# Idle matmuls, y on GpSimd, PSUM copies on ScalarE and reordered loads in an mLSTM cell followed by a max-out MLP

## The chip, the cores and the metric

The kernel runs on one core of a Trainium2 chip. Times are device microseconds of that core (us; ns where marked). A run is called fast or slow by its state: slow is a run more than 1.5% above the fastest run of the same kernel. Ratios are the mean time of one kernel's fast runs over that of the other's of the same rounds, so they are not quite the ratio of the medians that are quoted beside them. The ratios of the experiments leave out each kernel's profiled run and judge fast without it.

A matmul is called cold here when it runs at about half rate: 512-column matmuls then start about 427 ns apart, against about 216 ns warm. Some matmul records are missing from a trace, so a group of seven can stand for eight.

Engines are named as the profile names them: PE (TensorE matmuls), PEld (its weight loads), DVE (VectorE), ACT (ScalarE), POOL (GpSimd), SP (SyncE, which issues most DMAs here).

## The reference

There are two parts. The first is a recurrent attention cell (an mLSTM) for 4 batches, 8 heads, 768 steps and head size 40. Its output, reshaped to 3072 rows of 320, goes through a max-out MLP.

```python
for t in range(S):
    m_new = max(f_t + m, i_t)
    C = exp(f_t + m - m_new) * C + exp(i_t - m_new) * outer(v_t, k_t)
    n = exp(f_t + m - m_new) * n + exp(i_t - m_new) * k_t
    y_t = sigmoid(o_t) * (C @ q_t) / max(abs(n . q_t), 1)
x = y.reshape(3072, 320)
out = max(x @ w1, x @ w2) @ w_out          # w1, w2: 320x1024, w_out: 1024x320
```

## The kernel before

The kernel uses that the gates make the state constant after a short head of the sequence. It checks this on the data (`check_gates`) and would run a general version otherwise. Tokens are handled in 12 pairs of 128-token tiles. For each pair: q is cast to bf16 (`cast_q`), transposed on PE (`q_trans`), multiplied with the state (`h_pair`), scaled to y, and y is transposed (`y_trans`) to give xT. The MLP uses max(a, b) = relu(a - b) + b: `moe_u` multiplies xT with w1 - w2 and ACT takes the relu into `gt`; `moe_out` multiplies `gt` with w_out and adds xT times Wc = w2 @ w_out, which `w2_trans` and `wc_mm` prepare.

All instructions stand in the program's order on each engine. The parts that matter here:

```python
def h_pair(b, c0, P=None):                 # cut: ph = state x q on PE, two PSUM tiles
    for j in range(2):
        den = max(-ph[:, :, D], ...)       # DVE
        t = (sig + 1) * ph                 # DVE
        den = max(ph[:, :, D], den); rec = 1 / den                  # DVE
        nc.vector.tensor_tensor(out=y[:, j, 0:DM], in0=t, in1=rec, op=OP.mult)
    nc.vector.tensor_copy(out=y[:, :, DM:DM + 64], in_=y[:, :, DM - 64:DM])

def check_gates():                         # cut
    # DVE scan of f -> F; POOL a = i - F; DVE reduce of a; DVE ok_b
    nc.tensor.matmul(pf, ok_b, ones_b)     # PE: all 32 rows fine?
    # DVE: flag, flag_i

load_batch(1)                              # k, v, q, o of batch 1
...
cast_w2(0); cast_w2(1)                     # POOL
load_batch(2)                              # no store stands in the queue yet
...
load_batch(3)
...
for j, (g, half) in enumerate(steps):      # the loop: 10 steps, two outputs each
    moe_u(g, half, (2 + 2 * j, 3 + 2 * j))
    # y_trans of pair j+5; moe_out; h_pair of pair j+6; moe_out; q_trans of pair j+7
    # ACT: cast_q and gate_o of pair j+8
    if j == 4:
        check_gates()
```

PSUM tiles of the cell come from a pool of two buffers (`pp_f`), `gt` has two buffers, staged q and o have two buffers each.

Of the kernel before, what the change touches and what calls it, by code (L numbers as in the profile page):

```python
# [8 lines left out]
FP = mybir.dt.float32  # L9
BF = mybir.dt.bfloat16  # L10
# [7 lines left out]
def kernel(  # L18
# [100 lines left out]

    def load_qo(b, src, store, name, eng, rest):  # L120
        if b not in store:
            store[b] = stg.tile([128, H, NT, D], FP, name=name, tag=name)
        t = store[b]
        if not rest:
            eng.dma_start(out=t[:, :, 0, :], in_=src[b, :, 0:L, :].rearrange("h p d -> p h d"))
        else:
            eng.dma_start(out=t[:, :, 1:NT, :].rearrange("p h c d -> p h (c d)"),
                          in_=src[b, :, L:S, :].rearrange("h (p c) d -> p h (c d)", c=REST))

# [38 lines left out]
    def state_k(b):  # L168
        pk = pp_f.tile([3 * D, 3, SR], BF, name="pk", tag="pf")
        for tr in range(3):  # L170
            nc.tensor.transpose(pk[:, tr, :], kblk[:, b, tr].rearrange("p a b -> p (a b)"), ident_b[0:SR, 0:SR])  # L171
        kT[b] = ewp.tile([3 * D, 3, SR], BF, name="kT", tag="kT", bufs=2)
        nc.vector.tensor_copy(out=kT[b], in_=pk)

# [27 lines left out]
    def h_pair(b, c0, P=None):  # L202
# [15 lines left out]
        for j in range(2):  # L218
            c, ph = c0 + j, phs[j]
            den = ewp.tile([128, H], FP, name="den", tag="den")  # L220
            if c == 0:
                nc.vector.scalar_tensor_tensor(out=den, in0=ph[:, :, D], scalar=-1.0,
                                               in1=flT[:, b * H:(b + 1) * H], op0=OP.mult, op1=OP.max)
            else:
                nc.vector.tensor_scalar(out=den, in0=ph[:, :, D], scalar1=-1.0, scalar2=2.0,
                                        op0=OP.mult, op1=OP.max)
            t = ewp.tile([128, H, D], FP, name="t", tag="t")
            nc.vector.scalar_tensor_tensor(out=t, in0=sig[b][:, c], scalar=1.0, in1=ph[:, :, 0:D],  # L228
                                           op0=OP.add, op1=OP.mult)
            nc.vector.tensor_tensor(out=den, in0=ph[:, :, D], in1=den, op=OP.max)  # L230
            rec = ewp.tile([128, H], FP, name="rec", tag="rec")
            nc.vector.reciprocal(out=rec, in_=den)  # L232
            nc.vector.tensor_tensor(out=y[:, j, 0:DM].rearrange("p (h d) -> p h d", d=D), in0=t,  # L233
                                    in1=rec.unsqueeze(2).to_broadcast([128, H, D]), op=OP.mult)
        nc.vector.tensor_copy(out=y[:, :, DM:DM + 64], in_=y[:, :, DM - 64:DM])
        return y
# [5 lines left out]

    def y_trans(n0, y):
        g = group_of[n0]
        s0, m = n0 - GROUPS[g][0], GROUPS[g][1]
        if g not in xT:
            xT[g] = xtp.tile([128, 3, m * L], BF, name="xT", tag="xT")
        py = pp_f.tile([128, 3, 2 * L], BF, name="py", tag="pf")
        for j in range(2):
            for c in range(3):  # L250
                nc.tensor.transpose(py[:, c, j * L:(j + 1) * L], y[:, j, c * 128:(c + 1) * 128], ident_b)  # L251
        nc.vector.tensor_copy(out=xT[g][:, :, s0 * L:(s0 + 2) * L], in_=py)  # L252

# [58 lines left out]
    def diff_x(half):  # L312
        s = slice(half * 512, half * 512 + 512)
        for r in (slice(0, 64), slice(64, 128)):
            nc.vector.tensor_tensor(out=wd2[r, s], in0=wx_st[half, 0], in1=wx_st[half, 1], op=OP.subtract)

# [9 lines left out]
    def w2_trans():  # L326
        for c in range(2):
            pw = pp_o.tile([128, NFF, 128], BF, name="pw", tag="po")
            for f in range(NFF):
                nc.tensor.transpose(pw[:, f, :], w2b[:, c, f * 128:(f + 1) * 128], ident_b)  # L330
            nc.vector.tensor_copy(out=w2T[:, c], in_=pw)
        pw = pp_f.tile([128, NFF, 64], BF, name="pwx", tag="pf")
# [18 lines left out]
    def check_gates():  # L351
# [7 lines left out]
                                op0=OP.add, op1=OP.is_ge)  # L359
        nc.vector.tensor_tensor(out=ok_b, in0=viol[:, 1:2], in1=viol[:, 2:3], op=OP.mult)  # L360
        pf = pp_f.tile([1, 1], FP, name="pf", tag="pf")
        nc.tensor.matmul(pf, ok_b, ones_b, start=True, stop=True)
        nc.vector.tensor_scalar(out=flag, in0=pf, scalar1=BH - 0.5, scalar2=None, op0=OP.is_lt)
        nc.vector.tensor_copy(out=flag_i, in_=flag)



    nc.gpsimd.memset(kst[:, :, 2, :], 0.0)
    nc.gpsimd.memset(vst[:, :, 2, :], 0.0)
    nc.vector.memset(warm, 0.0)  # L370
    load_qo(0, q, qst, "qst", nc.scalar, False)
    load_qo(0, q, qst, "qst", nc.scalar, True)
    nc.scalar.activation(out=warm, in_=warm, func=AF.Exp)
    load_gates(0, L)
    load_kv(0, k, kst)
    load_kv(0, v, vst)
    load_qo(0, o_gate, ost, "ost", nc.sync, False)
    load_qo(0, o_gate, ost, "ost", nc.sync, True)
    for half in range(2):
        load_wx(half)  # L380
        load_w(half, 0)
        load_w(half, 1)
    wo_st = wst.tile([128, NFF, DM], FP, name="wo_st", tag="wo_st")
    nc.sync.dma_start(out=wo_st, in_=moe_w_out.rearrange("(f p) m -> p f m", p=128))

    def load_batch(b):
        load_kv(b, k, kst)
        load_kv(b, v, vst)
        for rest in (False, True):
            load_qo(b, q, qst, "qst", nc.sync, rest)  # L390
        for rest in (False, True):
            load_qo(b, o_gate, ost, "ost", nc.sync, rest)

    load_batch(1)
    load_gates(L, S)


    make_identity(nc, ident_b)
    make_identity(nc, ident_f)
    nc.vector.memset(one1, 1.0)  # L400
# [8 lines left out]
    nc.gpsimd.tensor_copy(out=bmk[:, 2, 1:3], in_=bm[:, 2, 0:2])  # L409
    nc.vector.memset(sel, 1.0)  # L410
    for base, cm, step, tstep in ((0, 1, -T0, 0), (T0 - 1, -1, T0, 0), (0, -1, T0, 1)):
        nc.gpsimd.affine_select(out=sel, in_=sel, compare_op=OP.is_ge, fill=0.0, base=base,
                                pattern=[[step, 3], [tstep, 128]], channel_multiplier=cm)

# [10 lines left out]
    cast_q(0, 0, 1, nc.scalar)  # L425
    prep_k(0, nc.vector)
    nc.vector.tensor_tensor(out=sel[:, 0], in0=sel[:, 0], in1=sel[:, 1], op=OP.max)
    nc.vector.tensor_tensor(out=mask, in0=sel[:, 0], in1=sel[:, 2], op=OP.max)
    state_k(0)
    pg = pp_f.tile([128, 2, BH], FP, name="pg", tag="pf")  # L430
# [6 lines left out]
    prep_v(0, nc.vector)  # L437
    state_c(0)


    cast_q(0, 1, 2, nc.scalar)
    q_trans(0, 0)
    P = scores(0)
    cast_q(0, 2, 4, nc.scalar)
    cast_q(0, 4, 6, nc.scalar)
    gate_o(0, 0, 1)
    gate_o(0, 1, 2)
    gate_o(0, 2, 4)
    gate_o(0, 4, 6)
    q_trans(0, 2)  # L450
    q_trans(0, 4)
    y0 = h_pair(0, 0, P)
    y1 = h_pair(0, 2)
    diff_x(0)
    y_trans(0, y0)
    diff(0, 0)
    diff(0, 1)
    y_trans(2, y1)
    y2 = h_pair(0, 4)
    moe_u(0, 0)  # L460
    y_trans(4, y2)
    diff_x(1)
    diff(1, 0)
    diff(1, 1)
    moe_u(1, 0)
    moe_u(0, 1)
    moe_u(1, 1)
    cast_w2(0)
    cast_w2(1)
    nc.vector.tensor_copy(out=wo, in_=wo_st)  # L470
    load_batch(2)
    prep_k(1, nc.gpsimd)
    prep_v(1, nc.gpsimd)
    cast_q(1, 0, 2, nc.scalar)
    cast_q(1, 2, 4, nc.scalar)
    cast_q(1, 4, 6, nc.scalar)
    gate_o(1, 0, 2)
    gate_o(1, 2, 4)
    gate_o(1, 4, 6)
    load_batch(3)  # L480
    w2_trans()
    wc_mm()
    state_k(1)
    state_c(1)
    q_trans(1, 0)
    open_outs((0, 1))
    moe_out(0)
    P = scores(1)
    q_trans(1, 2)
    y3 = h_pair(1, 0, P)  # L490
    moe_out(1)
    y4 = h_pair(1, 2)
    q_trans(1, 4)


    ys = {3: y3, 4: y4}
    cast_q(2, 0, 2, nc.scalar)
    y_trans(6, ys.pop(3))
    ys[5] = h_pair(1, 4)
    gate_o(2, 0, 2)  # L500
    y_trans(8, ys.pop(4))
    prep_k(2, nc.gpsimd)
    prep_v(2, nc.gpsimd)
    q_trans(2, 0)
    state_k(2)
# [4 lines left out]
    def place(p):  # L510
        return 2 * p // NT, 2 * p % NT

    steps = [(g, half) for g in range(2, len(GROUPS)) for half in range(2)]
    for j, (g, half) in enumerate(steps):
        moe_u(g, half, (2 + 2 * j, 3 + 2 * j))
        py_, ph_, pq_ = j + 5, j + 6, j + 7
# [7 lines left out]
        if pq_ < 12 and place(pq_)[1] == 0:  # L524
            state_k(place(pq_)[0])
        moe_out(2 + 2 * j)
        if ph_ < 12:
            ys[ph_] = h_pair(b, c, P)
        moe_out(3 + 2 * j)
        if pq_ < 12:  # L530
# [11 lines left out]
        if j == 4:  # L542
            check_gates()
    open_outs((22, 23))
    moe_out(22)
# [137 lines left out]
```

## Time and profile before

| | before |
|---|---|
| time, median of the first 3 runs | 141.1 us (140.52 to 147.07) |
| span of the profiled run | 139.7 us |
| PE, DVE, ACT, POOL busy | 97.0, 69.2, 51.3, 14.8 us |
| first wide expert matmul | 26.4 us |
| start of the loop | 61.4 us |
| end of the last matmul | 134.1 us |

The profiled run took 141.35 us.

The following lines are from the page of the kernel before: span, busy times, then four rows of 40 equal slices of the span (3.5 us each, counted from 0 in this text). Digits are tenths: the busy share of PE and DVE, the granted PE clock, and the mean busy share of the 16 DMA engines.

```profile
span 139.7 us, 2028 instructions
...
PE 97.0 (69%) x727; PEld 59.6 (43%) x735; DVE 69.2 (50%) x208; ACT 51.3 (37%) x82; POOL 14.8 (11%) x31
...
PE   0027532586678882579789999995059999999940
...
DVE  3455899939143599952726675748530640000000
...
PEclk9999999999999999658999999999955999999999
DMA  4949999896798981000021111112000112022221
...
```

PE is hardly busy in the first 8 us and has a hole at slice 28. The clock row dips twice: slices 16 to 18 (56 to 66 us) and 29 to 30 (101 to 108 us). DVE is at 9 in slices 5 to 7 (17 to 28 us) and 14 to 16 (49 to 59 us), where PE is not.

The next lines are from the windows view of the kernel before. After the window and its length stand busy time and count of PE, PEld, DVE, ACT and POOL, then clock, DMA share and GB/s.

```profile
...
15.00:26.00 11.00, 3.86 (x27) 2.38 (x28) 10.61 (x31) 0.02 (x1) 2.83 (x5) 1.00 1.03 296
47.00:61.00 14.00, 9.01 (x81) 6.51 (x81) 11.92 (x42) 3.36 (x6) 0.00 (x0) 0.87 0.40 116
...
```

DVE binds in both stretches: 10.6 of 11.0 us and 11.9 of 14.0 us.

From the wait table of the kernel before (engine, what it issued, whom it waited for: us in total, times, longest):

```profile
...
ACT gt L293 <- PE po L302: 14.0, 1, 14.0
...
PE pf L362 <- DVE ok_b L360: 6.2, 1, 6.2
...
```

ACT could not write `gt` because its buffer was still read by the matmuls of output 3, and PE stood 6.2 us before the flag matmul `pf`.

From the timeline of the kernel before, PE only (start, duration, engine, line, operation, tiles, count, and the idle time before with what ended it):

```profile
...
26.39 3.19 PE L278 MATMUL pu<-xT,wd 128*128 128x512 bf16 x7 [0.22 <-issue]
...
61.38 3.00 PE L278 MATMUL pu<-xT,wd 128*128 128x512 bf16 x7 [0.22 <-issue]
...
```

Seven 512-column matmuls take 3.19 us at 26.4 and 3.00 us at 61.4, about 430 to 460 ns each. In the warm part of the loop eight take about 1.9 us. Another window of the same timeline shows the gate check:

```profile
...
97.80 1.53 DVE L352 TENSOR_TENSOR_SCAN F<-one_100,F,f_sb 32x640 f32<-32x640 f32 x1
99.41 1.52 POOL L354 TENSOR_TENSOR a<-i_sb,F 32x640 f32<-32x640 f32 x1 [53.15 <-DVE F L352]
...
102.46 0.16 PE L362 MATMUL pf<-ones_b,ok_b 32*1 32x1 bf16 x1 [6.18 <-DVE ok_b L360]
...
103.38 2.77 PE L278 MATMUL pu<-xT,wd 128*128 128x512 bf16 x6 [0.22 <-issue]
...
```

The scan, POOL's subtraction and the reduction take from 97.8 to 102.3 us. PE stands meanwhile, and six wide matmuls after it take 2.77 us: the clock has fallen.

### The profile page before, as it was taken

What the parts mean: (1) busy time and instruction counts of PE and PEld (TensorE: products, weight loads), DVE (VectorE), ACT (ScalarE), POOL (GpSimd) and SP (SyncE); (2) the same over time, 40 slices, a digit from 0 to 9 for tenths busy, and PEclk for the clock granted to TensorE, in tenths of its full rate; (3) what the DMA queues carried; (4) which work ended last, traced back from release to release, by engine and by line L of the source; (5) the groups of instructions that cost most, each with busy time, mean ns of one, the idle gap of its engine ahead of it and who ended that gap; (6) DMA issues with size and microseconds to landing.
All of it is one profiled execution on the core that took longest, in us unless ns stands there. A gap on an engine that the chain in (4) does not pass through costs nothing.

```text
span 139.7 us, 2028 instructions
## 1 busy us (share of the span) xinstructions
PE 97.0 (69%) x727; PEld 59.6 (43%) x735; DVE 69.2 (50%) x208; ACT 51.3 (37%) x82; POOL 14.8 (11%) x31
## 2 busy tenths in 40 slices
PE   0027532586678882579789999995059999999940
PEld 0017312223256652444537565754023755666520
DVE  3455899939143599952726675748530640000000
ACT  4251300035467026000296746572003443654220
POOL 7300142500502200000000000000400000000000
PEclk9999999999999999658999999999955999999999
DMA  4949999896798981000021111112000112022221
GB/s 78 280 100 307 327 360 328 170 314 145 173 318 163 301 250 52 0 0 0 0 94 52 47 49 52 52 47 90 4 2 0 47 52 90 7 94 94 94 56 56
DMA packets 25840, 16.56 MB, mean 119 GB/s; under 512 B 12128, under 2 KB 24480, under 8 KB 25824
## 3 DMA queue, kind: packets, MB, share of 16 engines
q1 hardware_dynamic: 23744, 15.38, 38.7%
q10 hardware_dynamic: 2080, 0.98, 2.7%
q8 instruction: 8, 0.13, 0.5%
q14 instruction: 8, 0.07, 0.2%
HBM read 12.42 MB, written 3.93 MB: 117 GB/s over the span
## 4 chain that ended last, share of the span: by engine, by line
PE 57%; DVE 24%; ACT 5%; DMA 4%; issue 3%; POOL 2%; SPq 0%; DVEq 0%; ACTq 0%; POOLq 0%
PE pu L278 18%; PE po L302 16%; PE pu L284 5%; PE po L300 5%; DVE y L233 5%; ACT gt L293 5%; DVE t L228 4%; DMA kst<-in_k_dram 4%; PE pwc L342 2%; PE py L251 2%; PE pq L189 2%; DVE rec L232 2%; PE po L267 1%; DVE qT L191 1%; DVE xT L252 1%
## 5 line engine op out<-in xcount | busy, mean ns | idle before, releaser
L293 ACT ACTIVATE gt<-pu 128x1024 bf16<-128x1024 f32 (+1 forms) x28 | 23.7, 899 | 52.7 <-PE pu L284 38.6
L278 PE MATMUL pu<-xT,wd 128*128 128x512 bf16 (+1 forms) x104 | 27.0, 395 | 5.8 <-ACT gt L293 4.9
L302 PE MATMUL po<-wo,gt 128*128 128x320 bf16 x192 | 30.0, 299 | 0.0
L302 PEld LDWEIGHTS <-gt 128*128 128x128 bf16 x192 | 18.8, 98 | 7.5
L278 PEld LDWEIGHTS <-wd 128*128 128x128 bf16 x112 | 11.7, 108 | 16.6 <-issue 10.3
L304 ACT COPY o_sb<-po 128x320 f32<-128x320 f32 x24 | 10.1, 428 | 22.0 <-PE po L302 17.3
L252 DVE COPY xT<-py 128x768 bf16<-128x768 bf16 x12 | 6.7, 556 | 19.5 <-PE py L251 19.4
L233 DVE TENSOR_TENSOR y<-t,rec 128x320 bf16<-128x320 f32 x24 | 11.8, 492 | 0.8
L228 DVE SCALAR_TENSOR_TENSOR t<-sig,ph 128x320 f32<-128x320 f32 x24 | 11.4, 477 | 0.0
L300 PE MATMUL po<-Wc,xT 128*128 128x320 bf16 x48 | 10.8, 306 | 0.0
L251 PE MATMUL py<-ident_b,y 128*128 128x128 bf16 x72 | 7.5, 250 | 4.6 <-DVE den L230 3.3
L215 PE MATMUL ph<-cq,qT 120*128 120x123 bf16 (+1 forms) x60 | 6.3, 231 | 5.1 <-DVE xT L252 2.5
L155 ACT ACTIVATE sig<-ost 128x640 f32<-128x640 f32 (+1 forms) x13 | 8.6, 695 | 3.3 <-DMA ost<-in_o_gate_dram 3.3
L148 ACT CAST qb<-qst 128x640 bf16<-128x640 f32 (+1 forms) x13 | 8.5, 686 | 1.6 <-DMA qst<-in_q_dram 1.6
L189 PE MATMUL pq<-ident_b,qb 128*120 128x128 bf16 x72 | 7.4, 250 | 2.4 <-ACT sig L155 1.3
L251 PEld LDWEIGHTS <-y 128*128 128x128 bf16 x72 | 4.8, 110 | 9.0 <-DVE den L230 4.1
L284 PE MATMUL pu<-xT,wd_111 64*128 64x512 bf16 (+1 forms) x56 | 8.2, 374 | 0.0
L171 PE MATMUL pk<-ident_b,kblk 126*120 126x126 bf16 x12 | 1.7, 265 | 9.3 <-DVE kblk L159 8.8
L189 PEld LDWEIGHTS <-qb 128*120 128x120 bf16 x72 | 6.7, 161 | 3.1 <-ACT sig L155 1.4
L215 PEld LDWEIGHTS <-qT 120*128 120x128 bf16 x60 | 4.5, 106 | 6.9 <-issue 3.8
L354 POOL TENSOR_TENSOR a<-i_sb,F 32x640 f32<-32x640 f32 x1 | 1.5, 1521 | 53.1 <-DVE F L352 53.1
L191 DVE COPY qT<-pq 120x768 bf16<-120x768 bf16 x12 | 6.6, 552 | 0.6 <-PE pq L189 0.2
(91 smaller groups left out, 86.9 us busy)
## 6 DMA issues: line engine op xcount, KB each, us to landing
out_dram<-o_sb SPq DMA_DIRECT2D x24, 160.0 KB
ost<-in_o_gate_dram SPq DMA_DIRECT2D x4, 800.0 KB
qst<-in_q_dram SPq DMA_DIRECT2D x3, 800.0 KB
wo_st<-in_moe_w_out_dram SPq DMA_DIRECT2D x1, 1280.0 KB
qst<-in_q_dram ACTq DMA_DIRECT2D x1, 800.0 KB
ost<-in_o_gate_dram SPq DMA_DIRECT2D x4, 160.0 KB
w_0_144<-in_moe_w_dram SPq DMA_DIRECT2D x2, 256.0 KB
w_0_146<-in_moe_w_dram SPq DMA_DIRECT2D x2, 256.0 KB
```

Of the source, the lines that this page charges most:

```text
L155: nc.scalar.activation(out=sig[b][:, c0:c1], in_=ost[b][:, :, c0:c1, :].rearrange("p h c d -> p c h d"), func=AF.Tanh, scale=0.5)
L189: nc.tensor.transpose(pq[:, c, tr, :], qb[b][:, c0 + c, QH[tr]:QH[tr] + 3, :].rearrange("p a b -> p (a b)"), ident_b)
L215: nc.tensor.matmul(dst, qT[b][:, c, tr, :], cq[b][:, tr, 0:n * D1], start=True, stop=True)
L228: nc.vector.scalar_tensor_tensor(out=t, in0=sig[b][:, c], scalar=1.0, in1=ph[:, :, 0:D], op0=OP.add, op1=OP.mult)
L233: nc.vector.tensor_tensor(out=y[:, j, 0:DM].rearrange("p (h d) -> p h d", d=D), in0=t, in1=rec.unsqueeze(2).to_broadcast([128, H, D]), op= ...
L251: nc.tensor.transpose(py[:, c, j * L:(j + 1) * L], y[:, j, c * 128:(c + 1) * 128], ident_b)
L278: nc.tensor.matmul(pus[i // 2][:, i % 2, 0:n], wd[:, c, f * 128:(f + 1) * 128], x[:, c, :], start=(c == 0), stop=False)
L284: nc.tensor.matmul(pus[lo][:, j, 0:n], wd2[r, f * 128:(f + 1) * 128], x[r, 2, :], start=False, stop=True)
L293: nc.scalar.activation(out=gts[g][:, f:f + 2, :], in_=pus[lo][:, :, 0:n], func=AF.Relu)
L300: nc.tensor.matmul(po, xT[g][:, cc, s], Wc[:, cc, :], start=False, stop=False)
L302: nc.tensor.matmul(po, gts[g][:, f, s], wo[:, f, :], start=False, stop=(f == NFF - 1))
L304: nc.scalar.copy(out=o_sb, in_=po)
```

## The change

Its intent: keep the PE clock up while PE waits early on, by multiplying zeros; take y off DVE; spread the early PSUM copies over ACT; let what the first batch needs land first; and take the gate check's matmul out of PE's way. The diff, cut to its core:

```diff
-    def load_qo(b, src, store, name, eng, rest):
+    def load_qo(b, src, store, name, eng, c0, c1):     # any range of token tiles
@@ state_k
-        nc.vector.tensor_copy(out=kT[b], in_=pk)
+        nc.scalar.copy(out=kT[b], in_=pk)
@@ h_pair
-            nc.vector.tensor_tensor(out=y[:, j, 0:DM]..., in0=t, in1=rec..., op=OP.mult)
-        nc.vector.tensor_copy(out=y[:, :, DM:DM + 64], in_=y[:, :, DM - 64:DM])
+            nc.gpsimd.tensor_tensor(out=y[:, j, 0:DM]..., in0=t, in1=rec..., op=OP.mult)
+        nc.gpsimd.tensor_copy(out=y[:, :, DM:DM + 64], in_=y[:, :, DM - 64:DM])
@@ check_gates: its matmul and flag go to raise_flag(), called after the loop
+    def busy(n, cols):                                 # idle matmuls
+        z = pp_u.tile([128, 2, 512], FP, name="z", tag="pu")
+        for _ in range(n):
+            nc.tensor.matmul(z[:, 0, 0:cols], zero[:, 0:128], zero[:, 0:cols], start=True, stop=True)
@@ loads: batch 0 split into tiles 0, 1 to 3 and 4 to 5; o's head ahead of k
...
+    busy(16, 512)                                      # and 4, 4, 8, 8, 8 of 256 columns later
...
-    prep_k(0, nc.vector)
+    prep_k(0, nc.gpsimd)
...
     y2 = h_pair(0, 4)
+    cast_w2(0)                                         # POOL: now behind the third y
+    cast_w2(1)
...
-    load_batch(2)
...
-    load_batch(3)
...
     moe_out(1)
+    load_kvq(2)                                        # behind the stores of outputs 0 and 1
     ys = {3: h_pair(1, 0, P)}
...
+    moe_out(2)
+    load_o(2)
     ys[4] = h_pair(1, 2)
     q_trans(1, 4)
+    moe_out(3)
+    load_kvq(3)
     y_trans(6, ys.pop(3))
     ys[5] = h_pair(1, 4)
     cast_q(2, 0, 2, nc.scalar)
+    load_o(3)
     y_trans(8, ys.pop(4))
     prep_k(2, nc.gpsimd)
     prep_v(2, nc.gpsimd)
@@ loop: outputs 4 to 21 in ten steps, none in step 1
+    raise_flag()
```

More of the change, by code (lines that the diff above doesn't have):

```diff
@@ L123, in load_qo @@
         t = store[b]
-        if not rest:
+        if c0 == 0:
             eng.dma_start(out=t[:, :, 0, :], in_=src[b, :, 0:L, :].rearrange("h p d -> p h d"))
         else:
-            eng.dma_start(out=t[:, :, 1:NT, :].rearrange("p h c d -> p h (c d)"),
-                          in_=src[b, :, L:S, :].rearrange("h (p c) d -> p h (c d)", c=REST))
+            eng.dma_start(out=t[:, :, c0:c1, :].rearrange("p h c d -> p h (c d)"),
+                          in_=src[b, :, L:S, :].rearrange("h (p c) d -> p h (c d)", c=REST)
+                          [:, :, (c0 - 1) * D:(c1 - 1) * D])
     def load_wx(half):
@@ L232, in h_pair @@
             nc.vector.reciprocal(out=rec, in_=den)
-            nc.vector.tensor_tensor(out=y[:, j, 0:DM].rearrange("p (h d) -> p h d", d=D), in0=t,
+            nc.gpsimd.tensor_tensor(out=y[:, j, 0:DM].rearrange("p (h d) -> p h d", d=D), in0=t,
                                     in1=rec.unsqueeze(2).to_broadcast([128, H, D]), op=OP.mult)
-        nc.vector.tensor_copy(out=y[:, :, DM:DM + 64], in_=y[:, :, DM - 64:DM])
+        nc.gpsimd.tensor_copy(out=y[:, :, DM:DM + 64], in_=y[:, :, DM - 64:DM])
         return y
@@ L241, with copy, y_trans @@
     xT, gts = {}, {}
-    def y_trans(n0, y):
+    def copy(eng, out, in_):
+        (eng.copy if eng is nc.scalar else eng.tensor_copy)(out=out, in_=in_)
+    def y_trans(n0, y, eng=nc.vector):
         g = group_of[n0]
@@ L251, in y_trans @@
                 nc.tensor.transpose(py[:, c, j * L:(j + 1) * L], y[:, j, c * 128:(c + 1) * 128], ident_b)
-        nc.vector.tensor_copy(out=xT[g][:, :, s0 * L:(s0 + 2) * L], in_=py)
+        copy(eng, xT[g][:, :, s0 * L:(s0 + 2) * L], py)
     def where(n):
@@ L313, in diff_x @@
         s = slice(half * 512, half * 512 + 512)
-        for r in (slice(0, 64), slice(64, 128)):
-            nc.vector.tensor_tensor(out=wd2[r, s], in0=wx_st[half, 0], in1=wx_st[half, 1], op=OP.subtract)
+        nc.vector.tensor_tensor(out=wd2[0:64, s], in0=wx_st[half, 0], in1=wx_st[half, 1], op=OP.subtract)
+        nc.vector.tensor_copy(out=wd2[64:128, s], in_=wd2[0:64, s])
     def diff(half, c):
@@ L330, in w2_trans @@
                 nc.tensor.transpose(pw[:, f, :], w2b[:, c, f * 128:(f + 1) * 128], ident_b)
-            nc.vector.tensor_copy(out=w2T[:, c], in_=pw)
+            copy(nc.scalar if c else nc.vector, w2T[:, c], pw)
         pw = pp_f.tile([128, NFF, 64], BF, name="pwx", tag="pf")
@@ L360, in check_gates, with raise_flag @@
         nc.vector.tensor_tensor(out=ok_b, in0=viol[:, 1:2], in1=viol[:, 2:3], op=OP.mult)
+    def raise_flag():
         pf = pp_f.tile([1, 1], FP, name="pf", tag="pf")
@@ L364, in check_gates @@
         nc.vector.tensor_copy(out=flag_i, in_=flag)
-    nc.gpsimd.memset(kst[:, :, 2, :], 0.0)
-    nc.gpsimd.memset(vst[:, :, 2, :], 0.0)
+    def busy(n, cols):
+        z = pp_u.tile([128, 2, 512], FP, name="z", tag="pu")
+        for _ in range(n):
+            nc.tensor.matmul(z[:, 0, 0:cols], zero[:, 0:128], zero[:, 0:cols], start=True, stop=True)
+    zero = const.tile([128, 512], BF, name="zero")
+    nc.vector.memset(zero, 0.0)
     nc.vector.memset(warm, 0.0)
-    load_qo(0, q, qst, "qst", nc.scalar, False)
-    load_qo(0, q, qst, "qst", nc.scalar, True)
+    nc.vector.memset(kst[:, :, 2, :], 0.0)
+    nc.vector.memset(vst[:, :, 2, :], 0.0)
+    load_qo(0, q, qst, "qst", nc.scalar, 0, 1)
+    load_qo(0, q, qst, "qst", nc.scalar, 1, 4)
     nc.scalar.activation(out=warm, in_=warm, func=AF.Exp)
     load_gates(0, L)
+    load_qo(0, o_gate, ost, "ost", nc.sync, 0, 1)
     load_kv(0, k, kst)
     load_kv(0, v, vst)
-    load_qo(0, o_gate, ost, "ost", nc.sync, False)
-    load_qo(0, o_gate, ost, "ost", nc.sync, True)
+    load_qo(0, o_gate, ost, "ost", nc.sync, 1, 4)
     for half in range(2):
@@ L382, with load_kvq, load_o @@
         load_w(half, 1)
+    load_qo(0, q, qst, "qst", nc.sync, 4, NT)
+    load_qo(0, o_gate, ost, "ost", nc.sync, 4, NT)
     wo_st = wst.tile([128, NFF, DM], FP, name="wo_st", tag="wo_st")
     nc.sync.dma_start(out=wo_st, in_=moe_w_out.rearrange("(f p) m -> p f m", p=128))
-    def load_batch(b):
+    def load_kvq(b):
         load_kv(b, k, kst)
         load_kv(b, v, vst)
-        for rest in (False, True):
-            load_qo(b, q, qst, "qst", nc.sync, rest)
-        for rest in (False, True):
-            load_qo(b, o_gate, ost, "ost", nc.sync, rest)
-    load_batch(1)
-    load_gates(L, S)
+        load_qo(b, q, qst, "qst", nc.sync, 0, 1)
+        load_qo(b, q, qst, "qst", nc.sync, 1, NT)
+    def load_o(b):
+        load_qo(b, o_gate, ost, "ost", nc.sync, 0, 1)
+        load_qo(b, o_gate, ost, "ost", nc.sync, 1, NT)
+    load_kvq(1)
+    load_o(1)
     make_identity(nc, ident_b)
-    make_identity(nc, ident_f)
     nc.vector.memset(one1, 1.0)
@@ L409 @@
     nc.gpsimd.tensor_copy(out=bmk[:, 2, 1:3], in_=bm[:, 2, 0:2])
-    nc.vector.memset(sel, 1.0)
-    for base, cm, step, tstep in ((0, 1, -T0, 0), (T0 - 1, -1, T0, 0), (0, -1, T0, 1)):
-        nc.gpsimd.affine_select(out=sel, in_=sel, compare_op=OP.is_ge, fill=0.0, base=base,
-                                pattern=[[step, 3], [tstep, 128]], channel_multiplier=cm)
+    make_identity(nc, ident_f)
+    busy(16, 512)
     nc.vector.tensor_tensor_scan(out=F[:, 0:L], data0=ones[:, 0:L], data1=f_sb[:, 0:L], initial=0.0,
@@ L425 @@
     cast_q(0, 0, 1, nc.scalar)
-    prep_k(0, nc.vector)
-    nc.vector.tensor_tensor(out=sel[:, 0], in0=sel[:, 0], in1=sel[:, 1], op=OP.max)
-    nc.vector.tensor_tensor(out=mask, in0=sel[:, 0], in1=sel[:, 2], op=OP.max)
-    state_k(0)
+    prep_k(0, nc.gpsimd)
+    nc.vector.memset(sel, 1.0)
+    for base, cm, step, tstep in ((0, 1, -T0, 0), (T0 - 1, -1, T0, 0), (0, -1, T0, 1)):
+        nc.gpsimd.affine_select(out=sel, in_=sel, compare_op=OP.is_ge, fill=0.0, base=base,
+                                pattern=[[step, 3], [tstep, 128]], channel_multiplier=cm)
     pg = pp_f.tile([128, 2, BH], FP, name="pg", tag="pf")
@@ L437 @@
     prep_v(0, nc.vector)
-    state_c(0)
+    state_k(0)
+    nc.vector.tensor_tensor(out=sel[:, 0], in0=sel[:, 0], in1=sel[:, 1], op=OP.max)
+    nc.vector.tensor_tensor(out=mask, in0=sel[:, 0], in1=sel[:, 2], op=OP.max)
     cast_q(0, 1, 2, nc.scalar)
     q_trans(0, 0)
+    cast_q(0, 2, 4, nc.scalar)
+    gate_o(0, 0, 1)
+    state_c(0)
+    busy(4, 256)
     P = scores(0)
-    cast_q(0, 2, 4, nc.scalar)
-    cast_q(0, 4, 6, nc.scalar)
-    gate_o(0, 0, 1)
+    q_trans(0, 2)
     gate_o(0, 1, 2)
     gate_o(0, 2, 4)
-    gate_o(0, 4, 6)
-    q_trans(0, 2)
-    q_trans(0, 4)
+    busy(4, 256)
     y0 = h_pair(0, 0, P)
+    busy(8, 256)
     y1 = h_pair(0, 2)
     diff_x(0)
-    y_trans(0, y0)
+    busy(8, 256)
+    y_trans(0, y0, nc.scalar)
     diff(0, 0)
+    busy(8, 256)
+    y_trans(2, y1, nc.scalar)
     diff(0, 1)
-    y_trans(2, y1)
-    y2 = h_pair(0, 4)
+    cast_q(0, 4, 6, nc.scalar)
+    gate_o(0, 4, 6)
+    diff_x(1)
     moe_u(0, 0)
-    y_trans(4, y2)
-    diff_x(1)
+    q_trans(0, 4)
     diff(1, 0)
     diff(1, 1)
-    moe_u(1, 0)
-    moe_u(0, 1)
-    moe_u(1, 1)
+    y2 = h_pair(0, 4)
     cast_w2(0)
     cast_w2(1)
-    nc.vector.tensor_copy(out=wo, in_=wo_st)
-    load_batch(2)
+    moe_u(0, 1)
+    nc.vector.tensor_copy(out=wo[:, 0:4], in_=wo_st[:, 0:4])
+    nc.scalar.copy(out=wo[:, 4:8], in_=wo_st[:, 4:8])
+    y_trans(4, y2)
     prep_k(1, nc.gpsimd)
     prep_v(1, nc.gpsimd)
+    w2_trans()
+    moe_u(1, 0)
+    wc_mm()
+    moe_u(1, 1)
     cast_q(1, 0, 2, nc.scalar)
-    cast_q(1, 2, 4, nc.scalar)
-    cast_q(1, 4, 6, nc.scalar)
     gate_o(1, 0, 2)
-    gate_o(1, 2, 4)
-    gate_o(1, 4, 6)
-    load_batch(3)
-    w2_trans()
-    wc_mm()
     state_k(1)
     state_c(1)
+    cast_q(1, 2, 4, nc.scalar)
+    gate_o(1, 2, 4)
     q_trans(1, 0)
@@ L489 @@
     q_trans(1, 2)
-    y3 = h_pair(1, 0, P)
     moe_out(1)
-    y4 = h_pair(1, 2)
+    load_kvq(2)
+    ys = {3: h_pair(1, 0, P)}
+    cast_q(1, 4, 6, nc.scalar)
+    gate_o(1, 4, 6)
+    open_outs((2, 3))
+    moe_out(2)
+    load_o(2)
+    ys[4] = h_pair(1, 2)
     q_trans(1, 4)
-    ys = {3: y3, 4: y4}
-    cast_q(2, 0, 2, nc.scalar)
+    moe_out(3)
+    load_kvq(3)
     y_trans(6, ys.pop(3))
     ys[5] = h_pair(1, 4)
-    gate_o(2, 0, 2)
+    cast_q(2, 0, 2, nc.scalar)
+    load_o(3)
+    load_gates(L, S)
     y_trans(8, ys.pop(4))
@@ L503 @@
     prep_v(2, nc.gpsimd)
+    gate_o(2, 0, 2)
     q_trans(2, 0)
@@ L511, in place @@
         return 2 * p // NT, 2 * p % NT
+    outs = list(range(4, 22))
     steps = [(g, half) for g in range(2, len(GROUPS)) for half in range(2)]
     for j, (g, half) in enumerate(steps):
-        moe_u(g, half, (2 + 2 * j, 3 + 2 * j))
+        ns = [] if j == 1 else [outs.pop(0) for _ in range(2)]
+        moe_u(g, half, ns)
         py_, ph_, pq_ = j + 5, j + 6, j + 7
@@ L525 @@
             state_k(place(pq_)[0])
-        moe_out(2 + 2 * j)
+        if ns:
+            moe_out(ns[0])
         if ph_ < 12:
             ys[ph_] = h_pair(b, c, P)
-        moe_out(3 + 2 * j)
+        if ns:
+            moe_out(ns[1])
         if pq_ < 12:
```

## The prediction

> **What bounds the kernel now.** The page gives a span of 139.7 us with PE busy 97.0. The chain of waits and the timeline divide it:
> - 0 to 8.1 us: waiting for the k load (kst).
> - 8 to 26.4: a DVE/PE chain; in 15-26 DVE is busy 10.6 of 11.0. The first expert matmul starts at 26.4 and runs cold: its 512-column matmuls are about 427 ns apart, against about 216 in steady state.
> - 26.4 to 47: PE, relu and Wc preparation.
> - 47 to 61.4: DVE bound (11.9 of 14); the PE clock falls to 0.87, then 0.83.
> - 61.4 to 134.2: the loop, PE bound, about 6.3 us a warm step. Lost there: cold matmuls at 61-65 (about 1.5 us); gt waits for a buffer that output 3 still reads, PE stalls until 70.8 (about 2); PE waits for ok_b at 98-102.5 (about 4.5 of the 6.2 that the wait table lists); cold again 103-109 (about 3).
> - A tail of 5.5 us.
>
> "TensorE: Matmul & The Clock Gate", Part 1, of the Trainium skill says an idle window of about 3.4 us halves the PE clock and a busy one restores it. The trace agrees: 427 against 216 ns, and slow stretches follow the holes at 50 and 98 us. The granted-clock row does not show the cold start; the spacing does.
>
> **What the change does, costed.**
> 1. Filler matmuls (16x512, then 28x256) let the early chain and the first expert block run warm: that block goes from 3.96 to about 2.3 us, small matmuls save 0.2-0.3 per group. Gain 3-4 us.
> 2. y (0.49 us) and its copy (0.2, twice 0.92) leave DVE: 1.3 us per pair, visible only at 15-26 and 47-61. On POOL one y should take about 0.75 us (kblk, 360 wide, took 0.79 on POOL, 0.53 on DVE; "GPSIMD Engine Reference", section 3.1, says about 2x, the trace 1.5x). kT, xT and w2T copies on ACT help the same stretches.
> 3. Smaller q and o heads let k land 0.5-1 us earlier. First expert block at 19-20.5 instead of 26.4.
> 4. Given back: the w2 casts queue on POOL behind the third y (about 27), so w2 transposes wait until about 30; kT behind relus on ACT costs 1-2 us near 38-41. Output 0's matmuls end near 43 against 48.8; the loop starts near 53 against 61.4, with two more outputs done (2.7 us of PE).
> 5. Loop: no gt stall, no check hole, no cold restarts, two outputs fewer: 72.7 us becomes about 59 + 2-3 of small stalls.
> 6. Batches 2 and 3 load behind the first stores, about 42-57, just in time.
>
> Last PE work 53 + 61 = 114; tail 5.5; span about 119; reported time is about 1 us above the span: **119.5 us**, 8 in 10 between 115 and 124.5. Chances: faster by over 2% 0.97, within 2% 0.02, slower 0.01.
>
> **What would show it right.** 512-column matmuls at about 216 ns already at 20 us; DVE busy down by 14 us, POOL up by 20; no PE wait on ok_b around j=4 and no clock dip there; loop start near 53; no 14 us wait of ACT gt for output matmuls; the w2b casts late on POOL with PE waiting for them around 28-30.
>
> **What would make it wrong.** Fillers that do not keep the clock up, or dips in the holes at 28-30 and 38-41; POOL's y stretched to 1.4 us or more by DVE sharing SBUF (kblk showed 1.43 once), stalling y transposes every step; late batch-2 loads, stalling ACT in order; the check chain on DVE (4.5 us) delaying later PSUM copies so that the hole only moves.

## The result and the profile after

The changed kernel takes 125.11 us (median of 4, 124.66 to 126.19) against 140.81 (median of 4, 140.05 to 147.07) before. The ratio of the fast runs is 0.891 (95% interval 0.882 to 0.900). It is clearly faster, but slower than the range that was forecast, 115 to 124.5. A repeat (run c1 below) gave 125.49.

The same rows of the page of the changed kernel; a slice is now 3.1 us:

```profile
span 123.0 us, 2155 instructions
...
PE 100.0 (81%) x776; PEld 61.4 (50%) x783; DVE 49.5 (40%) x167; ACT 56.7 (46%) x90; POOL 36.9 (30%) x66
...
PE   5987958484996997518998899999995999999930
...
DVE  3337993951333276703363546361848000000000
...
PEclk9999999999599999995999999999999999999999
DMA  3979999939700023997998003020211111221320
...
```

DVE's busy time fell by 19.7 us and POOL's rose by 22.1. The clock row no longer dips around the gate check; it dips at slices 10 and 18 (31 to 34 and 55 to 58 us). PE has gaps at slices 16 and 17 (49 to 55 us), and DMA stands idle at slices 11 to 13 (34 to 43 us) before it is at 9 again from slice 16 on. From the wait table of the changed kernel:

```profile
...
PE pq L191 <- ACT qb L150: 4.8, 3, 3.2
...
```

The 14 us wait of ACT for `gt`'s buffer and the wait for `ok_b` are gone. The wait of this line is new. The timeline of the changed kernel, first the sixteen fillers at the start and then 18 to 31 us:

```profile
...
1.25 6.50 PE L378 MATMUL z<-zero 128*128 128x512 bf16 x16 [1.25 <-DVE warm L382]
...
18.72 1.89 PE L283 MATMUL pu<-xT,wd 128*128 128x512 bf16 x7 [0.89 <-ACT xT L246]
...
28.33 0.40 PE L335 MATMUL pw<-ident_b,w2b 128*128 128x128 bf16 x4 [1.15 <-POOL w2b L329]
...
28.78 1.03 POOL L329 CAST w2b<-w_1_158 128x1024 bf16<-128x1024 f32 x1
...
29.87 0.84 PE L335 MATMUL pw<-ident_b,w2b 128*128 128x128 bf16 x12 [1.14 <-POOL w2b L329]
...
30.98 1.89 PE L283 MATMUL pu<-xT,wd 128*128 128x256 bf16 x8
...
```

The first expert block starts at 18.7 us, warm (7 matmuls in 1.89 us), instead of 26.4 and cold. PE then waits twice for the w2 casts on POOL, 2.3 us together, and the eight 256-column matmuls after it take 1.89 us instead of the 1.04 that eight take at full clock later: the clock fell in the hole (slice 10 of the clock row). From 43 to 57 us:

```profile
...
43.00 2.23 SPq L314 DMA_DIRECT2D out_dram<-o_sb  x2
...
45.28 1.32 SPq L118 DMA_DIRECT2D kst<-in_k_dram  x3
...
48.41 0.58 SPq L128 DMA_DIRECT2D qst<-in_q_dram  x1
...
54.01 0.72 ACT L150 CAST qb<-qst 128x640 bf16<-128x640 f32 x1 [4.04 <-DMA qst<-in_q_dram]
...
54.79 0.84 PE L191 MATMUL pq<-ident_b,qb 128*120 128x128 bf16 x6 [3.17 <-ACT qb L150]
...
57.07 2.29 PE L283 MATMUL pu<-xT,wd 128*128 128x512 bf16 x7 [0.22 <-issue]
...
```

SP's queue is in order: it holds the store of output 1, which waits for the matmuls, then six small k and v loads and two q loads, each 0.4 us to issue. The rest of q is issued at 48.4 and lands 5.5 us later. ACT has waited 4.0 us for it, PE 3.2 us for ACT, and the first matmuls of the loop, at 57.1, are partly cold: seven took 2.29 us. The stretch of the gate check:

```profile
...
88.42 1.53 DVE L357 TENSOR_TENSOR_SCAN F<-one_100,F,f_sb 32x640 f32<-32x640 f32 x1
88.59 1.45 POOL L237 COPY y<-y 128x128 bf16<-128x128 bf16 x1
...
90.03 1.53 POOL L359 TENSOR_TENSOR a<-i_sb,F 32x640 f32<-32x640 f32 x1
...
92.96 0.54 DVE L246 COPY xT<-py 128x768 bf16<-128x768 bf16 x1
...
93.55 0.31 PE L217 MATMUL ph<-cq,qT 120*128 120x123 bf16 x3 [1.29 <-DVE xT L246]
...
```

POOL's small copy of y took 1.45 us beside DVE's scan; everywhere else in the loop it takes 0.29, and in e5, where the scan comes later, it takes 0.29 here too. The check's chain on DVE delays the copy of xT, which frees a PSUM buffer, and PE waits 1.3 us for it. Most of the hole of the kernel before is gone, and this part of it moved.

### The profile page after: what moved, and what is told of

It reads as the page before. It is cut to its first block, busy times and chain, and to the rows that moved or that the text cites. A ratio compares the mean times of both kernels' runs of the same rounds, so it can differ in the third digit from the quotient of the medians.

```text
span 123.0 us, 2155 instructions
## 1 busy us (share of the span) xinstructions
PE 100.0 (81%) x776; PEld 61.4 (50%) x783; DVE 49.5 (40%) x167; ACT 56.7 (46%) x90; POOL 36.9 (30%) x66
## 4 chain that ended last, share of the span: by engine, by line
PE 53%; DMA 17%; SPq 10%; POOL 6%; DVE 3%; ACT 3%; issue 2%; ACTq 0%; POOLq 0%
PE po L307 18%; PE pu L283 14%; DMA qst<-in_q_dram 8%; PE po L305 5%; SPq L118 5%; DMA wx_1_152<-in_moe_w_dram 5%; PE pu L289 4%; DMA vst<-in_v_dram 4%; PE pwc L347 3%; PE pq L191 3%; SPq L400 2%; PE py L256 2%; POOL w2b L329 2%; SPq L142 2%; PE po L272 1%
## 5 line engine op out<-in xcount | busy, mean ns | idle before, releaser
L235 POOL TENSOR_TENSOR y<-t,rec 128x320 bf16<-128x320 f32 x24 | 17.4, 741 | 53.1 <-DVE den L227 49.5
L283 PE MATMUL pu<-xT,wd 128*128 128x512 bf16 (+1 forms) x105 | 24.0, 364 | 2.6 <-ACT gt L298 1.2
L283 PEld LDWEIGHTS <-wd 128*128 128x128 bf16 x112 | 11.2, 103 | 11.1 <-issue 3.0
L246 DVE COPY xT<-py 128x768 bf16<-128x768 bf16 x10 | 5.5, 551 | 16.4 <-PE py L256 16.4
L378 PE MATMUL z<-zero 128*128 128x256 bf16 (+1 forms) x48 | 10.8, 380 | 1.3 <-DVE warm L382 1.3
L191 PE MATMUL pq<-ident_b,qb 128*120 128x128 bf16 x72 | 6.7, 230 | 6.2 <-ACT qb L150 4.8
L191 PEld LDWEIGHTS <-qb 128*120 128x120 bf16 x72 | 5.6, 138 | 7.7 <-ACT qb L150 5.3
L217 PE MATMUL ph<-cq,qT 120*128 120x123 bf16 (+1 forms) x60 | 5.8, 212 | 3.2 <-DVE xT L246 2.3
L378 PEld LDWEIGHTS <-zero 128*128 128x128 bf16 x48 | 5.1, 112 | 5.3 <-issue 3.8
L256 PE MATMUL py<-ident_b,y 128*128 128x128 bf16 x72 | 6.6, 221 | 1.2 <-POOL y L237 0.8
```

The lines of the kernel that those rows point to most:

```text
L191: nc.tensor.transpose(pq[:, c, tr, :], qb[b][:, c0 + c, QH[tr]:QH[tr] + 3, :].rearrange("p a b -> p (a b)"), ident_b)
L235: nc.gpsimd.tensor_tensor(out=y[:, j, 0:DM].rearrange("p (h d) -> p h d", d=D), in0=t, in1=rec.unsqueeze(2).to_broadcast([128, H, D]), op= ...
L256: nc.tensor.transpose(py[:, c, j * L:(j + 1) * L], y[:, j, c * 128:(c + 1) * 128], ident_b)
L283: nc.tensor.matmul(pus[i // 2][:, i % 2, 0:n], wd[:, c, f * 128:(f + 1) * 128], x[:, c, :], start=(c == 0), stop=False)
L378: nc.tensor.matmul(z[:, 0, 0:cols], zero[:, 0:128], zero[:, 0:cols], start=True, stop=True)
```

## The experiments

Twelve kernels ran, each on one chip with runs of the kernel before. All results were correct. Each experiment is an edit of the changed kernel.

| run | median us | ratio to before (95%) | fast runs of all |
|---|---|---|---|
| c1 changed kernel again | 125.49 | 0.899 (0.894 to 0.903) | 4 of 4 |
| e1 k, v, q of batch 2 early | 123.98 | 0.891 (0.887 to 0.895) | 4 of 4 |
| e2 also o early | 124.25 | 0.891 (0.887 to 0.894) | 4 of 4 |
| e3 fillers in the q wait | 124.36 | 0.894 (0.888 to 0.900) | 4 of 4 |
| e4 w2 casts early | 123.4 | 0.889 (0.882 to 0.897) | 4 of 4 |
| e5 check at step 6 | 124.38 | 0.886 (0.876 to 0.897) | 2 of 4 |
| e6 no fillers | 129.64 | 0.935 (0.927 to 0.944) | 3 of 4 |
| e7 y on DVE | 126.64 | none | 2 of 4 |
| e8 as e2, k and v of batch 2 prepared early | 120.12 | 0.864 (0.857 to 0.871) | 2 of 4 |
| e9 flag matmul inside | 131.35 | 0.943 (0.937 to 0.949) | 4 of 4 |
| e10 e8 + e4 + e5 | 118.0 | none | 1 of 4 |
| e11 e8 + half of e4 + e5 | 115.46 | 0.827 (0.823 to 0.832) | 5 of 5 |

Where runs of different calls are compared below, the ratios to before are compared, and one hundredth of a ratio is about 1.4 us.

### c1: the changed kernel again

> Control: the changed kernel unchanged, on the same chip as the three below. Every theory expects about 125 us, loop start (first 512-column expert matmul after the second batch) near 57, ACT idle about 4 us for the third batch's q near 50-54, and PE idle about 3.2 us there.

It took 125.49 us. In its profile PE waited 2.9 us for the q cast, the loop started at 57.5, and its first eight wide matmuls were cold throughout (3.62 us):

```profile
...
1.25 4.99 PE L378 MATMUL z<-zero 128*128 128x512 bf16 x16 [1.25 <-DVE warm L382]
...
57.52 3.62 PE L283 MATMUL pu<-xT,wd 128*128 128x512 bf16 x8
...
```

Here the first fillers took 4.99 us against 6.50, PE then waited 1.9 us for `kblk`, and the fillers at 12.4 us were cold again (four of 256 columns in 1.06 us instead of 0.60). The first expert block started at 20.0 us against 18.7: the same kernel differs by 1.3 us there from run to run.

### e1: k, v and q of batch 2 early

```diff
     cast_q(0, 4, 6, nc.scalar)
     gate_o(0, 4, 6)
+    load_kvq(2)
...
     moe_out(1)
-    load_kvq(2)
```

The place is the earliest that the two q buffers allow: batch 2 uses the buffer of batch 0, which is free after that cast. On SP's queue it stands behind the loads of batch 1.

> Only change: k, v and q of the third batch (batch 2) are issued on the SP queue right after the loads of batch 1 instead of behind the stores of outputs 0 and 1. Theory late-load: my prediction missed because these loads start only at 45 us behind two stores and q lands at 54, while the DMA engines idle from 34 to 43; with the load early, the ACT wait (4.0 us) and the PE wait (3.2 us) go, the first loop matmuls are warm, the loop starts near 53 and the time falls by about 4 us to 121. Rival serial-chain: the longer y path over POOL and the two PSUM buffers hold the loop start anyway; then the wait is renamed, the loop starts at 56 or later and the time falls by under 1.5 us. Rival bandwidth: the early load only delays batch 1's q and o, and the region around 38-43 grows by what is won.

It took 123.98 us, 1.5 less than c1 (the four runs of each do not overlap, the two intervals just do), far short of the 4 that the late-load theory expected. From its timeline:

```profile
...
51.24 1.40 POOL L235 TENSOR_TENSOR y<-t,rec 128x320 bf16<-128x320 f32 x2 [1.74 <-DVE den L227]
...
52.96 0.79 POOL L161 TENSOR_TENSOR kblk<-kst,bmk 126x360 bf16<-126x360 f32 x1
...
53.80 0.38 PE L173 MATMUL pk<-ident_b,kblk 126*120 126x126 bf16 x3 [1.54 <-POOL kblk L161]
...
55.02 3.51 PE L283 MATMUL pu<-xT,wd 128*128 128x512 bf16 x8
...
```

The q wait went as expected: the q transposes of batch 2 ran at 51.75 instead of 54.79 us. But PE then waited for the next operand. `kblk`, the block form of k, stands on POOL behind the two y of batch 1's last pair, although its data had long landed. "TensorE: Matmul & The Clock Gate" of the Trainium skill says in Part 1, under the engine queue depths, that each core of GpSimd takes its instructions strictly first in, first out; the trace agrees, `kblk` begins only when y and its copy are through, at 52.96. The loop began at 55.0, 2.1 us sooner than in the changed kernel's profile, but after this hole all eight matmuls were cold, 3.51 us, so 1.2 us of that were lost again. No single wait in this hole was longer than 1.54 us (the next, for `vw`, was 0.61, with small matmuls between), so the clock fell here without 3.4 us of idle time in one piece, which the prediction's rule speaks of. Both theories had a part: the load was late, and a second wait ended shortly behind it. The expectation named POOL's y path, and the step that held PE was the preparation queued behind it, not y itself. The bandwidth rival fell: output 0's matmuls ended at 42.4, as in the changed kernel.

### e2: o of batch 2 early too

```diff
+    load_kvq(2)
+    load_o(2)
...
     moe_out(2)
-    load_o(2)
```

> As e1, and o of batch 2 early as well. Late-load: as e1 (about 121), at best 0.3 us less, because o of batch 2 was 1 us behind q and would no longer be the next in line. Serial-chain: no further change, and little against the control.

It took 124.25 us, the same as e1. Its profile shows the same wait for `kblk` (1.5 us in one piece) and cold matmuls (3.44 us for eight). Its loop began at 56.2 us, but this profile was already 1.3 us behind e1's at the q transposes near 41 us, so that delay isn't put down to o.

### e3: the wait filled with idle matmuls

```diff
     y_trans(8, ys.pop(4))
+    busy(28, 256)
```

> The changed kernel with 28 more idle matmuls of 256 columns before the third batch's q transposes, which fill the PE's wait of 3.2 us without removing it. It splits the late-load cost into the wait and the cold clock after it: if the clock matters, matmuls from 55 to 59 run at about 216 ns instead of 427 and the time falls by 1 to 1.5 us; if only the wait matters, it stays within 0.3 us of the control. If the fillers themselves delay PE, it is slower.

It took 124.36 us, 1.1 below c1. From its timeline:

```profile
...
56.99 1.89 PE L283 MATMUL pu<-xT,wd 128*128 128x512 bf16 x8
...
```

The wait stays, the loop starts at 57.0, and its eight wide matmuls take 1.89 us where c1's took 3.62. The cold clock behind a hole therefore costs something over 1 us in itself; the intervals of c1 and e3 touch, so the size rests on the trace.

### e4: w2 casts ahead of the third y

```diff
-    y2 = h_pair(0, 4)
     cast_w2(0)
     cast_w2(1)
+    y2 = h_pair(0, 4)
```

> The changed kernel with the casts of w2 put on the POOL queue before the third y instead of behind it (POOL idles from 17.4 to 24.3 in the changed kernel). Theory given-back (point 4 of the prediction): PE's two waits for w2b (2.3 us) go, and the cold clock that follows (512- and 256-column matmuls at 31-35 us at half speed, about 1.5 us) goes too; output 0 ends 3 us sooner. Whether the total falls depends on the next wait: if the third batch's q still lands at 54 or a little earlier (it is issued after output 1's store, so it moves with it), the total falls by 2.5 to 3.5 us. If POOL's casts slow DVE through shared SBUF access, the third y comes later and the gain is under 1.5.

The ratio fell from 0.899 to 0.889, about 1.3 us, but the two intervals overlap a little, so the size is not certain. PE's two waits for `w2b` went, and output 0 ended at 40.7 instead of 42.5 us. The rest was given back, as its timeline shows:

```profile
...
17.33 3.28 DVE L323 TENSOR_TENSOR wd<-w,w 128x512 bf16<-128x512 f32 x2
...
18.48 1.03 POOL L329 CAST w2b<-w 128x1024 bf16<-128x1024 f32 x1
...
20.67 1.89 PE L283 MATMUL pu<-xT,wd 128*128 128x512 bf16 x4 [0.80 <-DVE wd L323]
...
26.79 1.98 POOL L235 TENSOR_TENSOR y<-t,rec 128x320 bf16<-128x320 f32 x2 [5.28 <-DVE den L227]
...
29.18 0.40 PE L256 MATMUL py<-ident_b,y 128*128 128x128 bf16 x4 [1.15 <-POOL y L237]
...
```

The two weight differences on DVE took 3.28 us while POOL cast, where they took 1.32 us in the changed kernel, and the third y came at 26.8 instead of 24.3, so that PE waited 1.15 us for it. "GPSIMD Engine Reference", section 1, says that GpSimd shares its SBUF interfaces with VectorE and that they contend when a DVE instruction has two SBUF inputs; a difference of two SBUF tiles is such an instruction, and the numbers agree. After that, q of batch 2 again ended the wait (3.4 us).

### e5: the gate check at step 6

```diff
-        if j == 4:
+        if j == 6:
             check_gates()
```

> The changed kernel with the gate check (a scan, a subtraction and a reduction) issued at loop step 6 instead of 4, where DVE has nothing left that PE needs. Theory moved-hole: the check's chain on DVE (88.4 to 93.0 us) delays the PSUM copies, which leaves PE idle for 1.3 us near 92-93.5; late, the time falls by 1 to 1.5 us. Rival: the hole is due to y on POOL, then no change.

The ratio is 0.886, about 1.7 us below c1's, but only two of four runs were fast and the intervals touch. The profile, which fell in a slow run, no longer has the 1.3 us wait of PE for that xT copy. The wait is shown to go; its worth in time is only indicated.

### e6: no fillers

```diff
-        for _ in range(n):
+        for _ in range(0):
```

> The changed kernel without any of its 44 idle matmuls. Theory: they are worth 3 to 4 us (point 1): without them the first expert block's 512-column matmuls at about 19 us take 427 ns instead of 216 and small matmuls are slower, output 0 ends 3 to 4 us later, total 128 to 129. Rival: other waits (DVE, POOL, loads) hide the clock, total within 1 us of 125.

The ratio rose to 0.935, about 5 us more than c1's (0.930 and about 4 us by its three fast runs alone). From its timeline, the first expert block:

```profile
...
19.86 1.01 PE L283 MATMUL pu<-xT,wd 128*128 128x512 bf16 x2 [0.89 <-ACT xT L246]
21.09 2.32 PE L283 MATMUL pu<-xT,wd 128*128 128x512 bf16 x5 [0.22 <-issue]
...
```

Cold matmuls again, 1.01 us for two and 2.32 for five, and the loop began at 60.5 instead of 57.1 or 57.5. The fillers are worth 3 to 5 us; the expectation was 3 to 4. They are not what moved the first expert block forward, though: without them it still starts at 19.9 us, against 26.4 before. The rest of the change did that (split loads, y on POOL, copies on ACT, the new program order), and of this only y was taken back in a run of its own (e7).

### e7: y back on DVE

```diff
-            nc.gpsimd.tensor_tensor(out=y[:, j, 0:DM]...
+            nc.vector.tensor_tensor(out=y[:, j, 0:DM]...
-        nc.gpsimd.tensor_copy(out=y[:, :, DM:DM + 64]...
+        nc.vector.tensor_copy(out=y[:, :, DM:DM + 64]...
```

> The changed kernel with y and its 64-column copy back on DVE. Theory: moving y to POOL pays only where DVE binds (12-15 and 43-52 us), and part of that is lost in POOL's longer latency; back on DVE the total rises by 1 to 2 us, DVE busy rises by about 14 us, POOL busy falls by 20. If the third batch's late q hides the second stretch, the rise is under 1 us. Rival: y on POOL is a cost in itself (0.74 against 0.49 us, shared SBUF access) and the total falls.

This is unclear: two fast runs, 124.28 and 125.69, two slow ones, and no interval. The two fast ones average 124.99 us, 0.899 of the fast runs of before, which is c1's ratio: no gain from y on POOL shows in the time of this kernel. The first expert block began at 21.7 us, later than with y on POOL (18.7 and 20.0), but this lead was gone at the loop. DVE busy rose to 64.6 us and POOL fell to 16.1, as expected. In this kernel the late q hides part of what the move could win: ACT's wait for q shrank to 3.4 us and the loop still began at 57.4. What y on POOL is worth in a kernel without that wait was not tried.

### e8: batch 2 early and prepared early

```diff
+    load_kvq(2)
+    load_o(2)
...
     prep_k(1, nc.gpsimd)
     prep_v(1, nc.gpsimd)
+    prep_k(2, nc.gpsimd)
+    prep_v(2, nc.gpsimd)
...
     y_trans(8, ys.pop(4))
-    prep_k(2, nc.gpsimd)
-    prep_v(2, nc.gpsimd)
```

> As e2 (k, v, q and o of batch 2 loaded early), and the block-diagonal k and the weighted v of batch 2 built on POOL right after those of batch 1, in POOL's idle time, instead of behind the y of batch 1's last pair. In e1's trace the q wait was gone, but PE then waited 1.5 us for kblk and 0.6 for vw, which stood on POOL behind two y and a copy, and all eight following 512-column matmuls ran cold (427 ns). Theory queue-of-waits: the late q was one of two waits that end almost together; with both gone the loop starts near 52.5 to 53, as the prediction said, its matmuls are warm, and the time is 120.5 to 121.5, some 4 us below the control's 125.5. Rival: a third wait (PSUM buffers, DVE) holds the start at 54.5 or later and the time at 123 or more.

It took 120.12 us, ratio 0.864 (0.857 to 0.871), about 5 us below c1 and clear of its interval. Two of the three runs behind this ratio are marked slow; the two fast runs alone average 118.97 us, 0.854 of before. From its timeline:

```profile
...
50.82 0.52 PE L191 MATMUL pq<-ident_b,qb 128*120 128x128 bf16 x6 [0.24 <-DVE den L232]
...
52.15 1.89 PE L283 MATMUL pu<-xT,wd 128*128 128x512 bf16 x8
...
```

The loop starts at 52.2 us and is warm from its first matmul (eight in 1.89 us). Two of its four runs are slow, 120.81 and 121.15 us at a granted clock of 0.95 to 0.97, against 118.51 and 119.42 at 0.986 to 0.992: the granted clock still differs from run to run, presumably by what it does in the remaining holes; the slow runs have no trace that would show it.

### e9: the flag's matmul inside the check

```diff
             check_gates()
+            raise_flag()
...
-    raise_flag()
     open_outs((22, 23))
```

> The changed kernel with the flag's matmul put back right behind the gate check in step 4, where the kernel before has it. Theory (point 5): PE is in order, so the matmul waits for ok_b and PE stalls about 4 us near 89-93; the clock may fall after it. Total 128 to 131. Rival: the check chain costs the same wherever the matmul stands, since DVE holds PE anyway; total within 1 us of 125.5.

The ratio rose to 0.943, about 6 us more than c1's. From its timeline:

```profile
...
93.88 0.16 PE L369 MATMUL pf<-ones_b,ok_b 32*1 32x1 bf16 x1 [5.17 <-DVE ok_b L365]
93.97 3.60 PE L283 MATMUL pu<-xT,wd 128*128 128x512 bf16 x8
...
```

PE stands 5.2 us before the flag's matmul, and the eight wide matmuls behind it are cold: 3.60 us. One instruction's place on an in-order engine was worth 6 us. With the fillers it is the largest part of the change that was measured.

### e10 and e11: the parts together

Both are e8 with e5. e10 puts both w2 casts ahead of the third y, e11 only the first:

```diff
+    cast_w2(0)
     y2 = h_pair(0, 4)
-    cast_w2(0)
     cast_w2(1)
```

> e8 with e4 (both w2 casts ahead of the third y on POOL) and e5 (gate check at step 6). If the gains add: 121 - 1.9 - 1.4 = 117.5 to 118. If w2 casts ahead of y only trade the wait for w2b against one for y (e4's trace: PE waits 1.15 us for the third y at 28-29), about 119.

> As e10, but only the first half of the w2 casts goes ahead of the third y. POOL's work of 1.6 us lands at 17 to 19 us, when POOL is idle, and the third y is not late. If the y wait of e4 came from the second half of the casts, this is faster than e10 by up to 1 us; if the casts slow DVE's weight differences either way, the two are the same within 0.5 us.

e10 gave 118.0 us with runs from 114.79 to 120.4, of which one counts as fast, so it has no ratio. Its profile fell in a slow run; there the loop started at 50.2 us but cold (3.47 us for eight). e11 gave 115.46 us, five runs between 115.28 and 116.21, all fast, ratio 0.827. From its page:

```profile
span 114.4 us, 2165 instructions
...
PEclk9999599999999999999999999999999999999998
...
```

The clock is full except in slice 4 (11 to 14 us). Its wait for w2 on PE is 0.9 us and the one for the third y 1.15; the loop starts at 51.3, warm. The third y was late after all, against the expectation: the two weight differences beside the one cast took 2.72 us, and y began at 25.6. e11's expectation, a gain of up to 1 us over e10, can't be judged on one fast run of e10. What is shown is that e11 beats both kernels, the changed one by a ratio of 0.827 / 0.899 = 0.92, and that all five of its runs are fast.

## Why the prediction was wrong

The direction, the size of the effect and most steps were right, but the time fell just outside the range. Step by step, from the profiled run:

| step | predicted us | measured us |
|---|---|---|
| first expert block starts | 19 to 20.5 | 18.7 |
| matmuls of output 0 end | near 43 | 42.5 |
| loop starts | near 53 | 57.1 |
| loop, to the end of the last matmul | 61 | 60.9 |
| tail to the end of the span | 5.5 | 5.0 |
| reported time above the span | about 1, not added | 1.7 |
| median above the profiled run | | 0.45 |

- **The step that failed is point 6**: "Batches 2 and 3 load behind the first stores, about 42-57, just in time." They were not in time. The load is issued behind the store of output 1 and six small loads, q lands at 54 us, PE waits 3.2 us, and the loop begins 4.1 us late with partly cold matmuls. The prediction named this risk ("late batch-2 loads, stalling ACT in order") and did not cost it, although the pieces stood in the trace of before: about 0.4 us per issue on SP, and 5 to 7 us for an 800 KB load to land (q issued at 1.3 us and waited for until 7.9, o issued at 7.9 and waited for until 13.3). e8 removes the wait together with the one behind it, and the loop then starts at 52.2, near the 53 that had been forecast, at 120.1 us. e1 shows that the load alone does not do it: the next wait, for POOL's `kblk`, let the loop begin only 2 us sooner than the first did.
- **The sum was also short.** 53 + 61 + 5.5 is already 119.5 for the span. The microsecond for the reported time was named and not added, and it is 1.7 (124.66 against 123.0), as it was in the kernel before (141.35 against 139.7). With 1.7 us added, the sum for a loop start of 53 is about 121, within the stated range.
- **Point 1** (fillers, 3 to 4 us) was right to slightly small: e6 gives 3 us at the loop start and 4 to 5 in the time. The kernel has 32 small fillers and 48 in all, not the 28 and 44 that the prediction and e6's expectation count. "Fillers that do not keep the clock up" came true in part: the clock fell at 31 us in the hole of the w2 casts, and in c1 also near 12 us.
- **Point 2** was right in its durations: a y on POOL took 741 ns on average against the 0.75 us forecast. DVE's relief was 19.7 us, more than the 14 named, because other work left it as well. In single profiles it moved the first expert block forward by 1.7 to 3 us; that it is worth anything in the whole time is not shown (e7).
- **Point 3** was right: `kblk` began at 7.1 us (7.5 in c1) instead of 8.2, and the first expert block at 18.7 (20.0 in c1) against a forecast of 19 to 20.5.
- **Point 4** was right in its sizes: PE waited 2.3 us for the w2 casts between 27 and 30 us, and 1.3 us near 40. That second wait was for ACT's q cast and not for kT, which the prediction named. The cold matmuls behind the first hole were not costed.
- **Point 5** was right: e9 shows 6 us for the flag's matmul alone, and no wait for `gt`'s buffer remains. Part of the check hole moved, 1.3 us, as the last risk said.
- **Not taken apart**: the change saves 15.7 us between the medians. The flag's place (e9, 6 us) and the fillers (e6, 4 to 5) are shown by runs. No run took back the split loads, the copies on ACT or the new order of the early program, which puts two more outputs ahead of the loop; what each of these is worth isn't shown.

## What to carry to other kernels

When a wait is removed, look for the wait that ends next behind it, on every engine that feeds the same instruction: a late load and a preparation queued in order behind unrelated work hid each other here. Removing the first alone gave 1.5 us, removing both about 5. Loads that wait for nothing should not stand behind stores that do, in one in-order queue; the DMA engines idled 9 us ahead of the load that was missed. A hole on PE can cost more than its length: here the cold matmuls after it added 1.2 to 1.7 us (e1, e3, e9). So an instruction whose result nobody needs soon, like a check's flag, belongs at the end of PE's queue.

## What the Trainium skill lacked or had wrong

- "TensorE: Matmul & The Clock Gate", Part 1, gives a warm-up of about 3.4 us, the transition varying by 0.5 us, and says that the count of cold matmuls differs from run to run. The spread of the time was larger here, and the measurement decides. The sixteen first fillers took between 4.99 us (c1) and 6.50 us (the changed kernel's profile). At 427 ns cold and about 216 ns warm that is an estimated 7 to 14 cold fillers, or 3 to 6 us before the clock rose, on the same instructions.
- The same page says that zero operands do not trip the peak-current limiter, and does not say whether they count as activity for the clock. They do: the first expert block was warm behind them and cold without them (e6), and 28 of them held it over a hole of about 3 us (e3, eight wide matmuls in 1.89 us instead of 3.62).
- The same page, Part 4, says that the full clock does not engage for PE transposes. Here six q transposes (transposes in the kernel, MATMUL in the trace) took 0.52 us in warm stretches and 0.84 to 0.90 us right behind a hole, so they ran at both rates like other matmuls, against the page. Whether transposes alone would raise the clock no run shows.
- "GPSIMD Engine Reference", section 3.1, measures a two-input operation, 2048 wide, at 1.96 times VectorE's time. For y, 320 wide, it was 741 against 492 ns, 1.5 times.
